# Linear attention and token/channel mixer on one core: another order of the first batches' operations, loads and constants

## The chip, the core and the metric

The kernel runs on one core of a Trainium2 chip. The metric is the device time of one execution in microseconds (us). The engines are TensorE (PE, with its weight loads PEld), VectorE (DVE), ScalarE (ACT), GpSimd (POOL) and SyncE (SP). Each takes its instructions in the order in which they were written, and a semaphore wait in front of one instruction holds everything behind it on that engine. DMAs are issued by SP (hardware queue, q1 in the profile) and POOL (software queue, q0 in the profile), and run on 16 DMA engines.

## What is computed

Cosformer attention over 8 batches, 8 heads, 576 positions and 64 channels a head, then one mixer layer:

```python
def phi(x, c, s):
    r = np.maximum(x, 0.0)
    return np.concatenate([r * c, r * s], axis=-1)
q_p, k_p = phi(q, cos_w, sin_w), phi(k, cos_w, sin_w)
kv = einsum('bhsf,bhsd->bhfd', k_p, v);  z = sum(k_p, axis=2)
x = einsum('bhsf,bhfd->bhsd', q_p, kv) / (einsum('bhsf,bhf->bhs', q_p, z) + 1e-06)
h = np.maximum(xt @ w_tok1, 0.0) @ w_tok2     # token mixing, xt = x transposed
u = x + h.transpose(0, 2, 1)
out = u + np.maximum(u @ w_ch1, 0.0) @ w_ch2  # channel mixing
```

## The kernel before

The 576 positions of a batch lie on 128 partitions, in J = 4 full row groups and a fifth, half-empty one (index 4); the half groups of two batches are put together in `u_tail` and go through the channel layer in pairs at the end. Work on heads is split in two halves of four heads, g = 0 and 1; g = 2 means both.

The stages of one batch, by the names of the operation list:

- `feat.b.t.j.g.f.E` (L289): one feature, relu(x * cos) or relu(x * sin) (f), of q or k, row group j, on engine E (D is DVE, A is ACT).
- `turn.b.i.g` (L305) transposes q's features on PE for two row groups (i = 0, 1) or for the fifth (i = 2), and `turno` (L314) copies them out of PSUM. Later batches use a DMA transpose instead, `turnx` (L319), issued by SP.
- `cast` (L300) rounds v to bf16 on DVE, ACT or POOL (P). `kvm` (L333) multiplies k's features with v, `kvo` copies the product out.
- `num` (L364) multiplies q's transposed features with kv; `numo` (L385) divides by the denominator on DVE (`x_out`, L373: a reciprocal and a multiplication) and gives x. From batch 2 on both heads' halves go together (`numf`, `numfo`).
- `mix` (L399) is the first token matmul, `mixo` its relu. `ux`, `ut`, `uto` (L414, L420) give u transposed; `um`, `uo` (L429, L436) give u itself, `tm`, `to` the fifth group's. `ubc`, `utr`, `utx` transpose u of later batches.
- `up` (L478) is the first channel matmul, in twelve blocks of columns, `upo` its relu; `dnw`, `dnj` the second, `o` (L508) adds u, and stores after every second row group.
- Loads: `ld.b.t.g.gate` (L220) issues two DMAs on SP, after the landing of the DMA that the gate names (v01 is v of batch 0, heads' half 1). The weights go through POOL's queue: `wt1` (w_tok1), `wt2` (w_tok2), `wu` (columns of w_ch1), `wd` (rows of w_ch2); `w2a` spreads w_tok2 to its place.

Batches 0, 1 and parts of 2 and 3 run by a list written out by hand or by a planner: `PLAN` (L16 to L55), a string of operations in program order, which the loop at L605 calls one after the other. The order of two operations on one engine is their order in the list. Ahead of the list stand the loads of batch 0 (L153: q, k, v's first half, v's second half), the memsets of constants, the sine and cosine tables, and 20 matmuls on zeros (`keep_warm`, L189) that keep PE busy while the first loads are under way. Behind the list come six rounds of `channel` for batches 2 to 7, with the attention of the next batches hooked in between, and one for the half groups of all pairs (`u_tail`).

Buffers that matter here: q and k each have two raw buffers (batches alternate), v has one; the features `qp` and `kp` have one buffer; PSUM has two slots of two banks (psA) and four of one (psM).

Of the kernel before, what the change touches and what calls it, by code (L numbers as in the profile page):

```python
# [681 lines left out]
```

## Time and profile before

| | us |
|---|---|
| median of 3 runs | 276.39 (275.82 to 276.94) |
| the profiled execution | 275.82 |
| its span, first to last instruction | 274.1 |
| PE busy | 260.9 (95% of the span) |
| DVE, ACT, POOL busy | 170.7, 114.4, 51.2 |
| first real transpose on PE | 8.88 |
| kvm of batch 0 starts | 17.63 |
| first mix of batch 0 | 21.54 |
| first `up` of batch 0 | 29.13 |
| kvm of batch 1, first half | 42.81 |
| last matmul ends | 270.43 |

The page gives the busy time of each engine, a strip of 40 slices of 6.85 us with busy tenths, the granted PE clock and the DMA share, then the chain that ended last, and the costliest groups of instructions. The trace behind it answers in more detail: a table by stretches of time, the waits of an engine with what ended them, the instructions in order of time, and the packets of each DMA queue in a stretch. An idle engine costs nothing unless it sets the end, so the strip is read first for the engine that is nearly always full, and then for where it is not.

### The profile page before, as it was taken

To read this page: it belongs to the slowest core of one execution; us is meant where nothing else is said; L and a number is where in the kernel's file an instruction comes from. 1 tells how busy PE (TensorE), PEld (TensorE's weight loads), DVE (VectorE), ACT (ScalarE), POOL (GpSimd) and SP (SyncE) were. 2 spreads that over 40 slices of the span, in tenths; PEclk is the share of its full clock that TensorE was granted. 3 is DMA by queue.
4 is the path that set the end of the run, shared out by engine and by line. 5 is a ranking of instruction groups with operands and counts; after the bars stand their busy time and mean duration, and the time that the engine had idled before them with its cause. 6 is when DMAs were issued, how large, how long until landed. Compare 5 with 4: busy or idle time off the path is not lost.

```text
span 274.1 us, 4680 instructions
## 1 busy us (share of the span) xinstructions
PE 260.9 (95%) x1846; PEld 134.5 (49%) x1846; DVE 170.7 (62%) x331; ACT 114.4 (42%) x181; POOL 51.2 (19%) x77
## 2 busy tenths in 40 slices
PE   7558999999999999999999999999999999999994
PEld 2257646445544554455445544554455444444443
DVE  4668889598773476947684869486738643323322
ACT  2653865377781339133913392338233201301300
POOL 5381060052030033600160017001100120000000
PEclk9959999999999999999999999999999999999999
DMA  6999999999899999999999968910990063003013
GB/s 204 332 151 258 311 199 218 366 356 202 256 256 200 362 366 363 152 230 281 347 158 266 306 215 137 250 57 1 177 243 4 2 124 125 0 17 138 0 44 110
DMA packets 79078, 53.36 MB, mean 195 GB/s; under 512 B 47824, under 2 KB 76496, under 8 KB 79056
## 3 DMA queue, kind: packets, MB, share of 16 engines
q1 hardware_dynamic: 74512, 48.77, 65.8%
q0 software_dynamic: 4144, 3.77, 9.4%
q10 hardware_dynamic: 400, 0.52, 0.5%
q8 instruction: 14, 0.23, 0.4%
q14 instruction: 8, 0.07, 0.1%
HBM read 35.85 MB, written 9.44 MB: 165 GB/s over the span
## 4 chain that ended last, share of the span: by engine, by line
PE 75%; DVE 0%; issue 0%
PE c_ps L562 26%; PE o_ps L579 26%; PE b L406 5%; PE c L485 4%; PE u L433 4%; PE o L497 4%; PE nf L357 3%; PE kv L327 3%; PE o_ps L571 1%; PE ut L461 1%; DVE u_tail L573 0%
## 5 line engine op out<-in xcount | busy, mean ns | idle before, releaser
L263 ACT ACTIVATE h<-c_ps 128x512 bf16<-128x512 f32 x52 | 31.0, 597 | 108.4 <-PE c_ps L562 64.2
L579 PE MATMUL o_ps<-wc,h 128*128 128x512 bf16 x324 | 71.9, 379 | 0.0
L562 PE MATMUL c_ps<-uT,wc 128*128 128x512 bf16 x288 | 70.4, 379 | 0.0
L579 PEld LDWEIGHTS <-h 128*128 128x128 bf16 x324 | 31.7, 98 | 38.2
L562 PEld LDWEIGHTS <-wc 128*128 128x128 bf16 x336 | 30.8, 98 | 32.6
L265 DVE TENSOR_SCALAR h<-c_ps 128x512 bf16<-128x512 f32 x32 | 22.0, 688 | 28.4 <-PE c_ps L562 28.4
L259 POOL CAST ub<-u 128x1024 bf16<-128x1024 f32 x14 | 15.1, 1076 | 124.4 <-DVE u L438 80.7
L582 DVE TENSOR_TENSOR u<-o_ps,u 128x512 f32<-128x512 f32 x24 | 16.5, 688 | 17.6 <-PE o_ps L579 17.6
L259 POOL CAST vbf<-vt 128x512 bf16<-128x512 f32 (+3 forms) x28 | 20.1, 753 | 22.3 <-PE c_ps L562 18.5
L296 ACT ACTIVATE qp<-qt,cos_t 128x512 bf16<-128x512 f32 x31 | 21.9, 713 | 5.0 <-DMA qt<-in_q_dram 5.0
L485 PE MATMUL c<-uT,wc 128*128 128x512 bf16 x96 | 23.1, 379 | 0.1
L497 PE MATMUL o<-wc,h 128*128 128x512 bf16 x96 | 22.3, 379 | 0.0
L296 ACT ACTIVATE qp<-qt,sin_t 128x512 bf16<-128x512 f32 x31 | 21.5, 711 | 0.7 <-DMA qt<-in_q_dram 0.7
L406 PE MATMUL b<-x,w 128*128 128x512 bf16 (+1 forms) x90 | 20.5, 355 | 1.0 <-DVE x L383 1.0
L383 DVE TENSOR_TENSOR x<-nf,den 128x512 bf16<-128x512 f32 x30 | 20.7, 691 | 1.0
L438 DVE TENSOR_TENSOR u<-u,x 128x1024 f32<-128x1024 f32 x16 | 19.4, 1220 | 1.7 <-PE u L433 1.7
L357 PEld LDWEIGHTS <-qpT 128*128 128x128 bf16 x320 | 15.4, 99 | 8.4 <-issue 0.4
L298 DVE TENSOR_SCALAR kp<-kt,cos_t 128x512 bf16<-128x512 f32 x30 | 17.9, 596 | 2.0 <-DMA kt<-in_k_dram 2.0
L298 DVE TENSOR_SCALAR kp<-kt,sin_t 128x512 bf16<-128x512 f32 x31 | 17.0, 557 | 0.0
L379 DVE TENSOR_SCALAR den<-nf 128x8 f32<-128x8 f32 x30 | 5.0, 166 | 18.4 <-PE nf L357 18.3
L433 PE MATMUL u<-B,w 128*128 128x512 bf16 x64 | 16.3, 379 | 0.0
L497 PEld LDWEIGHTS <-h 128*128 128x128 bf16 x96 | 9.0, 98 | 10.2
(89 smaller groups left out, 250.2 us busy)
## 6 DMA issues: line engine op xcount, KB each, us to landing
out_dram<-u SPq DMA_DIRECT2D x32, 256.0 KB, 2.6
qt<-in_q_dram SPq DMA_DIRECT2D x8, 640.0 KB, 8.6
kt<-in_k_dram SPq DMA_DIRECT2D x8, 640.0 KB, 7.2
qt<-in_q_dram SPq DMA_DIRECT2D x8, 512.0 KB, 7.5
kt<-in_k_dram SPq DMA_DIRECT2D x8, 512.0 KB, 6.0
vt<-in_v_dram SPq DMA_DIRECT2D x6, 640.0 KB, 9.2
vt<-in_v_dram SPq DMA_DIRECT2D x6, 512.0 KB, 8.1
wc<-in_moe_w_ch_dram POOLq DMA_DIRECT2D x4, 384.0 KB, 6.8
```

The source lines that it names most:

```text
L259: (nc.scalar.copy if eng == "A" else ENG[eng].tensor_copy)(dst, src)
L263: nc.scalar.activation(dst, src, AF.Relu)
L265: nc.vector.tensor_relu(dst, src)
L296: nc.scalar.activation(dst, src, AF.Relu, scale=tab)
L298: ENG[eng].tensor_scalar(dst, src, scalar1=tab, scalar2=0.0, op0=ALU.mult, op1=ALU.max)
L357: nc.tensor.matmul(nm[:, hh * (D + 1):(hh + 1) * (D + 1)], self.qpT[:, j * H + h, :], self.kv[:, h, :D + 1], start=(not eps or hh == 0), s ...
L406: nc.tensor.matmul(b1[:, mi], w1[:, col(self.c, j), mi * P:(mi + 1) * P], self.x[:, j, cs], start=(j == 0 and (g == 2 or mi == 0)), stop=( ...
L433: nc.tensor.matmul(ps[:, jj], w2[:, ki, 1 + 2 * g + jj, :], self.B1[:, ki, :], start=(ki == 0), stop=(ki == NT - 1))
L485: nc.tensor.matmul(ps, wc1[:, ki, mi * P:(mi + 1) * P], self.uT[:, :, ki, :], start=(ki == 0), stop=(ki == NCC - 1))
L497: nc.tensor.matmul(self.ps["o", j], self.h1[:, ki, j * P:(j + 1) * P], wc2[:, ki, :], start=(ki == 0), stop=(ki == NCH - 1))
L562: nc.tensor.matmul(c_ps, wc1[:, ki, mi * P:(mi + 1) * P], uT[:, :, ki, :], start=(ki == 0), stop=(ki == NCC - 1))
L579: nc.tensor.matmul(o_ps, h1[:, ki, j * P:(j + 1) * P], wc2[:, ki, :], start=(ki == 0), stop=(ki == NCH - 1))
```

## The change

The change gives the list another order, most of it in batches 0 and 1, and it moves constants and gates. Part by part:

- Ten memsets (`zero`, the clear of q's second buffer, `ones`, `eps_r`, two of `vbf`, two of `w1`, two of `w2`) go from POOL to DVE.
- The two index patterns (`iota`) are issued on POOL right after the first load; the identity is made where the list has the new word `mkid`.
- `ld.1.q.2` loses its gate v01 and stands first in the list, so SP issues it directly behind v of batch 0.
- w_tok2 comes first of the weights, gated by v01 (`wt2.v01`), behind one cast on POOL; w_tok1 follows after a second cast; then `wu.4`, `wu.0`, POOL's part of `w2a`, `wu.2`, `wu.8`.
- Batch 0's ten q features all come ahead of its k features, and its six groups of transposes ahead of `kvm.0.0`. Two features of batch 1's q stand on DVE ahead of `numo.0.0.1`.
- k of batch 1 is gated by `wu2` instead of q of batch 1. On POOL two `wd` are gated by k of batch 1, then one by `wu8`, one by v of batch 1; two casts of batch 1 follow. q of batch 2 comes before k.
- k of batch 4 is issued ahead of batch 3's DMA transposes; v of batch 4, and q gated by k of batch 3, ahead of the last stores of batch 1.

`FIRST = "S"` keeps batch 0's loads on SP; `ldp` is defined and not used. The diff, with the list up to batch 1's numerators and its last lines, first the old list:

```diff
-feat.0.q.2.2.0.D feat.0.q.0.2.1.D feat.0.q.1.2.0.A wt1.k02 feat.0.q.3.2.0.A feat.0.q.0.2.0.D feat.0.q.4.2.0.D
-feat.0.k.4.2.0.D wt2 feat.0.k.0.2.0.A feat.0.q.1.2.1.D turn.0.0.0 wu.4.4.k02 feat.0.k.4.2.1.D turn.0.0.1
-feat.0.k.2.2.1.A feat.0.k.0.2.1.D feat.0.k.1.2.1.A feat.0.q.4.2.1.D feat.0.k.3.2.0.A turn.0.2.0 turno.0.2.0.A
-turno.0.0.0.A cast.0.3.2.0.D feat.0.q.3.2.1.D feat.0.k.1.2.0.D feat.0.q.2.2.1.D turn.0.1.0 turno.0.1.0.A
-cast.0.0.3.0.P feat.0.k.3.2.1.D feat.0.k.2.2.0.D kvm.0.0 kvo.0.0.A cast.0.0.3.1.P cast.0.3.2.1.P kvm.0.1
-num.0.0.0 turno.0.0.1.D numo.0.0.0 w2a.0.A mix.0.0.0 num.0.1.0 w2a.1.P turn.0.1.1 num.0.2.0 ld.1.q.2.v01
-kvo.0.1.D num.0.0.1 turn.0.2.1 mix.0.1.0 wu.2.2.wt2 numo.0.1.0 turno.0.1.1.A mix.0.2.0 num.0.1.1 turno.0.2.1.A
-num.0.2.1 mix.0.3.0 numo.0.0.1 numo.0.2.0 mix.0.4.0 mixo.0.0.A wu.0.2.v01 wu.8.4 mix.0.0.1 feat.1.q.0.2.0.A
-numo.0.1.1 mix.0.1.1 ux.0.0 feat.1.q.0.2.1.A mix.0.2.1 mix.0.3.1 ux.0.3 numo.0.2.1 mix.0.4.1 ux.0.1 ut.0.1
-mixo.0.1.D ut.0.0 uto.0.0.A ut.0.3 um.0.0 feat.1.q.4.2.0.A feat.1.q.3.2.0.D feat.1.q.1.2.1.A uto.0.1.D
-up.0.2.0.2 up.0.3.0.2 feat.1.q.1.2.0.D ux.0.2 ut.0.2 turn.1.0.1 uo.0.0 feat.1.q.2.2.1.A ld.1.k.2.q12 uto.0.3.D
...
+ld.1.q.2 feat.0.q.4.2.0.D feat.0.q.1.2.0.A feat.0.q.4.2.1.D feat.0.q.2.2.1.A feat.0.q.0.2.0.D mkid
+feat.0.q.2.2.0.A feat.0.q.3.2.0.D feat.0.q.1.2.1.D feat.0.q.0.2.1.D turn.0.0.0 turn.0.2.1 feat.0.q.3.2.1.A
+feat.0.k.3.2.0.D turn.0.1.1 turno.0.1.1.D feat.0.k.4.2.0.A turn.0.2.0 feat.0.k.1.2.1.D feat.0.k.3.2.1.D
+turno.0.2.1.A cast.0.0.3.0.P wt2.v01 turn.0.0.1 turn.0.1.0 turno.0.0.0.A feat.0.k.2.2.0.A feat.0.k.0.2.1.A
+feat.0.k.4.2.1.D feat.0.k.2.2.1.D feat.0.k.0.2.0.A feat.0.k.1.2.0.D cast.0.3.2.0.D kvm.0.0 turno.0.1.0.D
+kvo.0.0.D num.0.1.0 turno.0.2.0.A num.0.2.0 numo.0.2.0 cast.0.0.3.1.P cast.0.3.2.1.A numo.0.1.0 num.0.0.0
+numo.0.0.0 kvm.0.1 kvo.0.1.D num.0.2.1 turno.0.0.1.A num.0.0.1 feat.1.q.1.2.0.D feat.1.q.2.2.1.A num.0.1.1
+feat.1.q.0.2.1.D wt1.k02 mix.0.0.0 wu.4.4.q02 numo.0.0.1 mix.0.0.1 mix.0.1.1 numo.0.1.1 mix.0.2.1 mix.0.3.1
+numo.0.2.1 wu.0.2.k02 mix.0.1.0 mix.0.2.0 feat.1.q.2.2.0.A mix.0.3.0 mix.0.4.0 ux.0.0 ux.0.1 mix.0.4.1 w2a.0.A
+mixo.0.1.A mixo.0.0.D w2a.1.P ut.0.0 uto.0.0.A tm.0 ux.0.2 to.0 ut.0.2 feat.1.q.1.2.1.A feat.1.q.0.2.0.D
+uto.0.2.D feat.1.q.3.2.1.D ut.0.1 uto.0.1.A um.0.0 uo.0.0 wu.2.2.v00 up.0.2.0.2 up.0.3.0.2 wu.8.4.v01 ux.0.3
+ut.0.3 turn.1.0.1 turno.1.0.1.D ld.1.k.2.wu2 feat.1.q.4.2.1.A feat.1.q.4.2.0.A turn.1.2.1 uto.0.3.A up.0.0.0.2
+up.0.2.2.4 up.0.3.2.4 up.0.8 upo2.0.1.D turno.1.2.1.A up.0.6 up.0.11 ld.1.v.0 upo.0.8.A ld.1.v.1.wu8
+feat.1.q.3.2.0.D up.0.4 upo.0.4.D feat.1.k.0.2.0.D feat.1.k.3.2.0.A up.0.1.0.2 up.0.0.2.4 feat.1.k.4.2.1.D
+upo.0.11.D feat.1.k.2.2.1.D upo.0.6.A wd.6.3.k12 feat.1.k.3.2.1.D up.0.1.2.4 upo2.0.0.D turn.1.1.1
+feat.1.k.1.2.1.A wd.0.3.k12 up.0.10 feat.1.k.1.2.0.A feat.1.k.2.2.0.D turn.1.0.0 feat.1.k.4.2.0.D wd.9.3.wu8
+um.0.1 cast.1.4.1.0.D feat.1.k.0.2.1.D wd.3.3.v11 upo.0.10.A turno.1.1.1.A turn.1.1.0 turno.1.1.0.A
+ld.2.q.2.wd0 turno.1.0.0.A up.0.5 upo.0.5.A cast.1.0.4.0.P cast.1.0.4.1.P turn.1.2.0 turno.1.2.0.D kvm.1.0
+kvo.1.0.A up.0.9 num.1.1.0 cast.1.4.1.1.P uo.0.1 ld.2.k.2.wd9 numo.1.1.0 kvm.1.1 up.0.7 upo.0.9.A kvo.1.1.A
...
+feat.3.k.3.2.0.A upo.1.8.A uo.2.1 ubc.2.1 feat.3.k.2.2.1.D feat.3.k.2.2.0.A cast.3.1.1.2.P dnj.1.3.0 dnj.1.2.0
+utx.2.1 dnj.1.3.1 dnj.1.2.1 feat.3.q.4.2.1.A turnx.3.4.1 dnj.1.0.1 o.1.0 dnj.1.1.0 dnj.1.1.1 cast.3.4.1.2.A
+ld.4.v.2 o.1.2 tm.2 ld.4.q.2.k32 o.1.3 to.2 o.1.1
...
-    nc.gpsimd.memset(zero, 0.0)
+    nc.vector.memset(zero, 0.0)
...
-    def load(b, t, hs=slice(0, H)):
+    def load(b, t, hs=slice(0, H), eng=nc.sync):
...
-            dmas.append(nc.sync.dma_start(
+            dmas.append(eng.dma_start(
...
-    for t, g in LOADS0:
-        d = load(0, t, heads(g))
+    for n, (t, g) in enumerate(LOADS0):
+        d = load(0, t, heads(g), nc.gpsimd if FIRST == "P" else nc.sync)
         landed[f"{t}0{g}"] = d[1]
...
+        if n == 0:
+            nc.gpsimd.iota(pos_i, pattern=[[2, JT]], base=-2, channel_multiplier=R)
+            nc.gpsimd.iota(par_i, pattern=[[0, 1]], base=0, channel_multiplier=1)
...
-    clear("q", 1, nc.gpsimd)
+    clear("q", 1, nc.vector)
...
-    make_identity(nc, ident)
...
-    nc.gpsimd.memset(ones, 1.0)
+    nc.vector.memset(ones, 1.0)
...
-    nc.gpsimd.memset(eps_r, 1e-6 / P)
+    nc.vector.memset(eps_r, 1e-6 / P)
...
-        nc.gpsimd.memset(t[:, :, :, D:], 1.0)
+        nc.vector.memset(t[:, :, :, D:], 1.0)
...
-        nc.gpsimd.memset(w1[:, i], 0.0)
+        nc.vector.memset(w1[:, i], 0.0)
...
-        nc.gpsimd.memset(w2[:, :, i, :], 0.0)
+        nc.vector.memset(w2[:, :, i, :], 0.0)
```

## The prediction

> **What bounds the kernel now.** I read the strip of 40 slices first, then the table by stage, the waits of PE, and the timeline of the first 30 us.
>
> ```profile
> PE   7558999999999999999999999999999999999994
> PEclk9959999999999999999999999999999999999999
> DMA  6999999999899999999999968910990063003013
> ```
>
> PE is full from the fifth slice on (about 27 us). Before it lie three poor slices, one of them at half clock. The DMA engines are full from the second slice to about 165 us, so early loads compete.
>
> ```profile
> 10.00:15.00 5.00, 1.23 (x16) 0.91 (x16) 4.36 (x8) 4.00 (x6) 3.76 (x5) 0.93 1.01 250
> 15.00:20.00 5.00, 3.20 (x51) 3.20 (x52) 3.49 (x5) 2.04 (x3) 4.05 (x5) 0.50 0.96 156
> 20.00:25.00 5.00, 3.95 (x74) 3.38 (x72) 3.86 (x11) 2.13 (x3) 1.71 (x3) 0.89 1.17 278
> 25.00:30.00 5.00, 4.85 (x38) 2.92 (x36) 4.10 (x8) 3.32 (x6) 0.00 (x0) 1.00 1.27 209
> ```
>
> Columns: stretch, its length, busy PE, PEld, DVE, ACT, POOL, clock, DMA share, GB/s. PE is idle for 3.77, 1.80, 1.05 and 0.15 us in these four, and the clock halves in the second. After 30 us PE loses about 0.3 us until the last store. So only the start can win, and all of it is won or lost by the moment at which PE becomes full.
>
> ```profile
> PE tr L311 <- DVE qp L298: 6.3, 3, 3.6
> PE b L406 <- DVE x L383: 1.0, 1, 1.0
> SPq L142 <- DMA qt<-in_q_dram: 11.9, 1, 11.9
> ```
>
> The first line is PE waiting for q features to transpose, the second the token mix waiting for x. The third is SP, between issuing batch 1's q (13.89 to 15.19) and its landing (27.1).
>
> ```profile
> 20.55 0.21 DVE L377 RECIPROCAL den<-nm 128x8 f32<-128x8 f32 x1 [2.06 <-PE nm L361]
> ...
> 22.24 0.21 DVE L377 RECIPROCAL den<-nm 128x8 f32<-128x8 f32 x1 [0.42 <-PE nm L361]
> ...
> 25.59 0.43 DVE L383 TENSOR_TENSOR x<-nm,den 128x256 bf16<-128x256 f32 x1
> ```
>
> The six normalisations (numo) of batch 0 are DVE's chain from 20.55 to 26.02. Each costs 0.88 us for two row groups (22.24 to 23.15, 24.54 to 25.39) and 0.54 for one. The mixes follow them; the last ends at 26.44 and `ut` starts at 26.66.
>
> **The change, part by part.**
>
> *Constants on VectorE.* Ten memsets leave POOL for DVE. DVE's rows are 0.48 us for 512 columns and 0.06 for one, so 0.0008 per column: zero 0.48, q's clear 0.48, ones 0.17, eps 0.06, vbf 2 x 0.13, w1 and w2 4 x 0.27, together 2.5 (2.7 by POOL's rows for the same memsets). DVE is idle for 2.63 us before q lands (6.93), which covers it; an overrun of 0.1 is taken up by the idle 2.04 us before k (10.64). `zero` comes 0.7 later, so the 20 warming matmuls end at 9.7 instead of 9.0. The first transposes need features that end at 9.5. Cost 0. If DVE's cover were gone, each 0.1 would move the q features, and those have 1 us to spare until k. The identity moves on POOL behind the iotas and is ready by about 2: 0.
>
> *All q features, then all transposes, first.* DVE: 6 x 0.42 from 6.93 = 9.5; ACT: 4 x 0.62 = 9.4. All 5 x 8 = 40 transposes are done by about 13.0 (the last two groups wait for PSUM slots freed by copies after k's landing). Of them 0.61 + 0.38 us ran at 22 to 23.4 before. What is late next is k. ACT has one k feature (11.35), two copies (0.5 and 1.0), three k features: 14.8. DVE has one k feature, a copy of 0.65, five k features and a cast.
>
> ```profile
> 12.23 0.48 DVE L298 TENSOR_SCALAR qp<-qt,sin_t 128x512 bf16<-128x512 f32 x1
> ...
> 15.70 1.04 DVE L298 TENSOR_SCALAR qp<-qt,sin_t 128x512 bf16<-128x512 f32 x1
> ...
> 14.63 2.58 POOL L259 CAST vbf<-vt 128x768 bf16<-128x768 f32 x3
> ```
>
> The same feature costs 0.48 alone and 0.83 to 1.04 beside POOL's casts. POOL casts twice instead of three times now; I charge 0.4 for each of three overlapped operations: DVE is done at 15.5. The Trainium skill, "SBUF — State Buffer", section "SBUF: two separate sides", calls the port pair of DVE and GpSimd an exclusive lock, where one side blocks wholly. By that rule an overlapped feature would wait out a whole cast of 0.86, which would put DVE's end near 16.8; the row shows less, and I go by the row.
>
> So kvm.0.0 ends at 16.0 instead of 18.9, kv is copied by 16.6, and the six num (0.66 us at half clock or 0.31 at full clock for two row groups) feed DVE from 17.2 (full clock) to 17.7 (half). DVE then has numo 0.54 + 0.88 + 0.88 and the kv copy 0.42: it is free at 19.9 to 20.4. Before, that point was 23.15. Gained so far: about 3 us of DVE's chain.
>
> *Batch 1's q loses its gate; weights come later.* This decides. In the new list, two features of batch 1's q stand on DVE directly ahead of numo.0.0.1, numo.0.1.1 and numo.0.2.1; whatever q1 is late by, those three, four mixes and everything behind on PE are late by. Let L be q1's landing. From L: two features 0.87, numo 0.88 and 0.88, two mixes 0.43, four mixes of group 0 0.86, two `ux` 0.44, one mix 0.22 = L + 4.58. Then 0.1 for B's last evacuation, and `ut`, `tm`, `ux`, `ut`, `ut`, `um` (0.43, 0.43, 0.22, 0.43, 0.43, 0.86 at full clock): the first channel matmul (`up`) starts at L + 7.5. The old kernel starts it at 29.13 without having done `tm`, so the same work stands at 29.13 + 0.43 = 29.56. Gain = 29.56 - 7.5 - L = 22.1 - L, and no more than 22.1 - 20.1 = 2.0, since DVE itself is free only at 20 or so.
>
> What is L? Before, q1 was issued at 13.89 into a queue full of weights:
>
> ```profile
> q0 software_dynamic: 98, 0.10, 65.6%
> q1 hardware_dynamic: 87, 0.09, 31.9%
> ```
>
> That is 19 to 20 us: packets, MB, share of 16 engines. Weights (q0) and loads (q1) go packet for packet, but a weight packet takes some 0.11 us and a load's 0.05; alone, loads do 335 packets per us (344 in 11 to 12). Now q1's 1056 packets (summed by one-us stretches, 17 to 27) stand directly behind v's, which end at 12.7. w2 waits for v's landing (13.2, my estimate; 13.8 before, with w1 in between), is issued 13.2 to 13.95, and its packets start at 14.3: q1 has 536 done. Beside w2's 256 packets 256 more (to 16.9), beside w1's 128 large ones (0.28 us each) 128 (to 19.5), the last 136 beside wu4 at 120 per us: 20.6. Tails of single engines cost up to 1 us more (k1: last bulk at 33.0, landed 34.4). L = 21.6: gain 0.5. Bounds: 20.1 (q1 gets ahead further) and 24.7 (as starved as before, when its first half landed).
>
> The Trainium skill speaks against expecting more here: "DMA: Bandwidth & Descriptors", section "Issuing engines are not separate DMA queues", says that DMAs of all issuing engines run on the same 16 engines and interleave. By that rule the reordering moves q1 forward only by moving weights back; by the rows the bytes until about 30 us are also the same.
>
> Are the weights late, then? w1 (issued 14.9 to 16.75 on POOL, behind one cast) ends at 19.5 and lands by about 20.3; the first mix wants it at 21 to 22. w2 lands at 17.5 and w2a has until 26. wu4 ends at 22.8, wu0 24.5, wu2 26.2 and lands by 27; up.0.2 wants it at 29.1 (27.6 at best). Nothing waits, with 0.6 to 2 us to spare.
>
> *Batch 1's list (30 to 62 us).* k1 waits for wu2 as above, is issued at 27 as before (27.18) and lands near 33.6. POOL's queue then has wd6, wd0, wd9, and wd3 waiting for v's second half, with both casts of v that kvm.1.0 and kvm.1.1 need behind it. v1 has 790 packets done when wd's come (34.6); 266 at 120 per us plus the tail: 38.2. wd3 39.0, cast 1.12: 40.1. kvm.1.0 comes one `up` (0.86) earlier in the list: 42.81 - 0.86 - 0.5 = 41.45. Spare 1.3 us: cost 0. The q2, k2, v2 loads come 0 to 3 us earlier: 0.
>
> *Batches 2 and 3, and the fifth batch's loads.* SP gets k's two issues ahead of batch 3's transposes (0.6 us each) and q's ahead of the last stores. Batch 3's transposes had been issued from 75.66 with 4.6 us to land, for a PE that wants them at 94.9: over 10 us to spare, cost 0. PE's work is the same matmuls, and it is full: 0.
>
> Sum: 0.5 us off the profiled execution (275.82 us, span 274.1). The median of the runs is 0.57 above that execution, so 276.39 - 0.5 = **275.9 us**.
>
> **Rivals.**
>
> 1. *q1 gets through early* (L at 20.1 to 20.8) and the clock stays up, since PE is busy 1.5 us between 11.2 and 14.6 instead of 1.2. Gain 1.3 to 2.0, and up to 0.3 where PE's late stalls go too: about 274.6. For it: loads alone at 335 per us. Against: 98 to 87 packets beside weights.
> 2. *q1 is starved as before.* From 13.9 to 17 q1 had no packets at all while weights flowed. If loads behind v stop when w2 starts and L is 24.7, the gain is 22.1 - 24.7 = -2.6: 279.0, slower. It decides from L = 23.5 on. Against: v's queue is already running then.
> 3. *A wait further on*: v's second half lands after 39.5, and POOL holds kvm.1.0's cast behind wd3; each us later costs one. If k1 starts 2 us later, v shares with all wd's, lands at 42, and the cast ends at 44: 2.5 lost, less 0.5: 278.4. For it: k2 before took 12.3 us to land beside wd's.
>
> **Numbers.** Faster or slower by over 0.5% (1.4 us) is about what a measurement can tell. Forecast 0.40 (275.0 to 277.8; its own range 275.2 to 276.6), rival 1 0.27, rivals 2 and 3 together 0.33. The range takes in rival 1 down to 274.0 and most of rivals 2 and 3: 274.0 to 279.0.
>
> **What would show it.** Right: q1 landing at 21 to 22.3, DVE waiting there for q1 by 1 to 2 us ahead of numo.0.0.1; transposes all before 13.5; first `up` near 28.6 to 29.1; no PE wait after. Wrong: w1 or wu2 ending a PE wait, POOL's cast ending kvm.1.0's wait, DVE still at memsets at 6.93.

## The result and the profile after

The changed kernel takes 277.69 us (median of 4 runs, 277.51 to 277.99) where the kernel before takes 276.38 beside it (275.82 to 276.94). The ratio is 1.0048, with a 95% interval of 1.0026 to 1.0071: slower by about 1.3 us, where the prediction had 0.5 us faster. The profiled execution of the changed kernel took 277.99 us, with a span of 276.2 (before: 275.82 and 274.1).

The strip of 40 slices of the changed kernel:

```profile
PE   6747996999999999999999999999999999999994
PEclk9995999999999999999999999999999999999999
DMA  6999999999999999999989887930890053003013
```

The half clock has moved by one slice, from the third to the fourth, and the seventh slice (41 to 48 us) now has a 6 where the old kernel had a 9. So there are two places to look at: the start, and something after 41 us. The table by stage, with the columns of the one shown before:

```profile
10.00:15.00 5.00, 2.97 (x51) 2.56 (x51) 4.26 (x8) 4.35 (x8) 1.85 (x2) 1.00 1.09 355
15.00:20.00 5.00, 2.42 (x68) 2.19 (x65) 4.21 (x11) 4.22 (x6) 4.98 (x8) 1.00 1.05 207
20.00:25.00 5.00, 3.48 (x37) 2.56 (x34) 3.09 (x8) 0.00 (x0) 1.49 (x3) 0.61 1.08 146
25.00:30.00 5.00, 5.00 (x30) 3.10 (x29) 1.91 (x4) 1.93 (x4) 0.00 (x0) 0.71 1.20 179
```

Between 10 and 15 us PE does more (2.97 us busy instead of 1.23), and at full clock. From 21.1 to 27.9 it runs at half clock, and that is where the matmuls of the token mix lie. The waits of PE between 9 and 50 us (times in us: total, count, longest):

```profile
PE nm L362 <- DVE kv L264: 2.3, 2, 1.8
PE kv L332 <- DVE kp L303: 2.3, 1, 2.3
PE b L411 <- DMA w<-in_moe_w_tok_dram: 1.5, 1, 1.5
...
PE tr L316 <- DVE qp L303: 0.6, 1, 0.6
```

The wait for q features has shrunk from 6.3 us to 0.6, as the reordering was to do. Two others have come in its place: the mixes wait 1.5 us for w_tok1, and kv of batch 1 waits 2.3 us for a k feature of DVE. PE's timeline has both, with their price:

```profile
19.77 0.29 PE L362 MATMUL nm<-kv,qpT 128*128 128x65 bf16 x4 [1.79 <-DVE kv L264]
...
22.19 4.00 PE L411 MATMUL b<-x,w 128*128 128x256 bf16 x18 [1.52 <-DMA w<-in_moe_w_tok_dram]
...
30.54 0.81 PE L490 MATMUL c<-uT,wc 128*128 128x512 bf16 x3
...
45.37 0.81 PE L332 MATMUL kv<-vbf,kp 128*128 128x65 bf16 x20 [2.28 <-DVE kp L303]
```

The first `up` (L490) stands at 30.54; the old kernel had the same work done at 29.56 (29.13 and 0.43 of `tm`, as in the prediction). So 0.98 us is lost by then in this execution (other executions of the same start are compared below). At kv of batch 1 the start is 2.56 us later than before (45.37 against 42.81), and at the first matmul of the later rounds (c_ps, L567) 2.21 us later (93.07 against 90.86). From there on the distance stays 2.2 until the last matmul (272.63 against 270.41): what the change does behind that point, the fifth batch's loads among it, costs and gains nothing.

### The profile page after: what moved, and what is told of

It is laid out like the page before. It is cut to its first block, busy times and chain, and to the rows that moved or that the text cites. A ratio compares the mean times of both kernels' runs of the same rounds, so it can differ in the third digit from the quotient of the medians.

```text
span 276.2 us, 4685 instructions
## 1 busy us (share of the span) xinstructions
PE 261.3 (95%) x1846; PEld 134.4 (49%) x1846; DVE 167.4 (61%) x333; ACT 116.4 (42%) x187; POOL 49.5 (18%) x69
## 4 chain that ended last, share of the span: by engine, by line
PE 88%; DMA 5%; DVE 4%; issue 1%; POOL 1%; SPq 0%; ACT 0%
PE c_ps L567 26%; PE o_ps L584 25%; PE o L502 8%; PE b L411 7%; PE c L490 6%; PE u L438 5%; PE kv L332 3%; DMA vt<-in_v_dram 3%; PE nf L362 3%; DMA w<-in_moe_w_tok_dram 2%; DVE kp L303 2%; PE ut L466 1%; PE o_ps L576 1%; PE uT L428 1%; DVE h L270 1%
## 5 line engine op out<-in xcount | busy, mean ns | idle before, releaser
L567 PE MATMUL c_ps<-uT,wc 128*128 128x512 bf16 x288 | 70.4, 379 | 0.0
L584 PEld LDWEIGHTS <-h 128*128 128x128 bf16 x324 | 31.7, 98 | 38.2
L567 PEld LDWEIGHTS <-wc 128*128 128x128 bf16 x336 | 30.8, 98 | 32.6
L264 POOL CAST ub<-u 128x1024 bf16<-128x1024 f32 x14 | 14.9, 1067 | 103.8 <-DVE u L443 54.8
L264 POOL CAST vbf<-vt 128x512 bf16<-128x512 f32 (+3 forms) x30 | 21.7, 757 | 50.9 <-DMA vt<-in_v_dram 39.9
L301 ACT ACTIVATE qp<-qt,sin_t 128x512 bf16<-128x512 f32 x32 | 22.6, 711 | 2.6 <-DMA qt<-in_q_dram 2.6
L411 PE MATMUL b<-x,w 128*128 128x512 bf16 (+1 forms) x90 | 22.2, 387 | 1.5 <-DMA w<-in_moe_w_tok_dram 1.5
L490 PE MATMUL c<-uT,wc 128*128 128x512 bf16 x96 | 22.7, 379 | 0.0
L301 ACT ACTIVATE qp<-qt,cos_t 128x512 bf16<-128x512 f32 x29 | 20.5, 711 | 3.9 <-DMA qt<-in_q_dram 3.9
L388 DVE TENSOR_TENSOR x<-nf,den 128x512 bf16<-128x512 f32 x30 | 20.7, 691 | 1.0
L362 PEld LDWEIGHTS <-qpT 128*128 128x128 bf16 x320 | 15.3, 98 | 10.5 <-issue 2.1
L303 DVE TENSOR_SCALAR kp<-kt,sin_t 128x512 bf16<-128x512 f32 x30 | 18.5, 629 | 0.0
L332 PE MATMUL kv<-vbf,kp 128*128 128x65 bf16 x320 | 12.0, 193 | 3.8 <-DVE kp L303 2.3
L303 DVE TENSOR_SCALAR kp<-kt,cos_t 128x512 bf16<-128x512 f32 x28 | 15.0, 544 | 0.8 <-DMA kt<-in_k_dram 0.8
```

The source lines that it names most:

```text
L264: (nc.scalar.copy if eng == "A" else ENG[eng].tensor_copy)(dst, src)
L301: nc.scalar.activation(dst, src, AF.Relu, scale=tab)
L303: ENG[eng].tensor_scalar(dst, src, scalar1=tab, scalar2=0.0, op0=ALU.mult, op1=ALU.max)
L362: nc.tensor.matmul(nm[:, hh * (D + 1):(hh + 1) * (D + 1)], self.qpT[:, j * H + h, :], self.kv[:, h, :D + 1], start=(not eps or hh == 0), s ...
L411: nc.tensor.matmul(b1[:, mi], w1[:, col(self.c, j), mi * P:(mi + 1) * P], self.x[:, j, cs], start=(j == 0 and (g == 2 or mi == 0)), stop=( ...
L490: nc.tensor.matmul(ps, wc1[:, ki, mi * P:(mi + 1) * P], self.uT[:, :, ki, :], start=(ki == 0), stop=(ki == NCC - 1))
```

## The experiments

All kernels ran beside the kernel before on their own chip, so ratios are compared. The kernel before had medians of 276.1 to 276.6 in the groups of runs, and of 275.46 in the one of `e9_front`, `e10_tail` and `e11_split`. The milestones come from one profiled execution each (us from the span's start): the first `up` of batch 0, the start of kv of batch 1, and the first c_ps. "After" is the time between first `up` and c_ps. The kernel before starts this stretch at 29.56; e4, e7, e9, e10, e13 and e14 have other work ahead of that `up` than the changed kernel, so theirs isn't given.

| kernel | median, us | ratio to before (95%) | first up | kv of batch 1 | c_ps | after |
|---|---|---|---|---|---|---|
| before | 276.38 | 1 | 29.13 | 42.81 | 90.86 | 61.30 |
| changed | 277.69 | 1.0048 (1.0026 to 1.0071) | 30.54 | 45.37 | 93.07 | 62.53 |
| e2_casts | 275.72 | 0.9987 (0.9968 to 1.0007) | 30.08 | 43.01 | 90.71 | 60.63 |
| e11_split | 276.45 | 1.0021 (1.0000 to 1.0041) | 29.50 | 44.09 | 91.79 | 62.29 |
| e10_tail | 277.95 | 1.0078 (1.0050 to 1.0107) | 30.01 | 44.73 | 92.44 | |
| e14_tail_casts | 276.77 | 1.0007 (0.9989 to 1.0024) | 31.49 | 43.97 | 91.87 | |
| e8_q1gated | 280.21 | 1.0138 (1.0115 to 1.0161) | 34.80 | 48.57 | 96.27 | 61.47 |
| e4_q1early | 275.50 | 0.9990 (0.9969 to 1.0010) | 28.57 | 42.25 | 90.13 | |
| e7_constants | 276.37 | 1.0008 (0.9991 to 1.0026) | 29.30 | 42.98 | 90.88 | |
| e3_w1first | 276.77 | 1.0030 (1.0013 to 1.0046) | 30.89 | 44.98 | 92.68 | 61.79 |
| e1_warm | 277.46 | 1.0049 (1.0022 to 1.0076) | 29.06 | 44.03 | 93.29 | 64.23 |
| e5_both | 276.23 | 1.0005 (0.9983 to 1.0028) | 28.61 | 41.91 | 90.64 | 62.03 |
| e6_swap_casts | 277.26 | 1.0040 (1.0017 to 1.0063) | 27.76 | 43.16 | 92.54 | 64.78 |
| e9_front | 278.17 | 1.0086 (1.0053 to 1.0119) | 31.55 | 44.15 | 92.09 | |
| e13_front_gates | 276.36 | 1.0004 (0.9986 to 1.0023) | 30.09 | 42.68 | 90.28 | |
| e12_inputs | 274.60 | 0.9935 (0.9913 to 0.9957) | 29.29 | 42.01 | 89.73 | 60.44 |
| e15_cold_inputs | 275.82 | 0.9992 (0.9973 to 1.0011) | 30.31 | 43.00 | 90.76 | 60.45 |
| e16_inputs_pool | 277.58 | 1.0046 (1.0024 to 1.0068) | 28.15 | 42.83 | 92.08 | 63.93 |

The theory at the outset had two parts: the wait at kv of batch 1 comes from POOL's casts of v, which hold up DVE's k feature, and the late start comes from w_tok1's landing and the half clock that follows. The rival was that the start is all, and the wait further on only a consequence.

### The wait at kv of batch 1

DVE, POOL and PE of the changed kernel around 40 us; the first line is the one feature that matters:

```profile
40.06 2.72 DVE L303 TENSOR_SCALAR kp<-kt,sin_t 128x512 bf16<-128x512 f32 x1
```

```profile
39.70 0.77 POOL L248 DMA_DIRECT2D wc<-in_moe_w_ch_dram  x1 [1.38 <-DMA vt<-in_v_dram]
40.48 2.57 POOL L264 CAST vbf<-vt 128x1024 bf16<-128x1024 f32 x3
```

The same feature takes 0.48 us a moment earlier. POOL waits for v's second half, issues its last w_ch2 load at 39.70 (0.77 us) and then casts twice 1024 columns, until 42.50; the feature ends at 42.79. The k features queued behind it end at 45.31, and kv starts at 45.37.

**e2_casts** takes only those two casts from POOL, to places where ACT is idle.

```diff
-... upo.0.5.A cast.1.0.4.0.P cast.1.0.4.1.P turn.1.2.0
+... feat.1.k.1.2.0.A cast.1.0.4.0.A feat.1.k.2.2.0.D ... wd.3.3.v11 cast.1.0.4.1.A upo.0.10.A ... upo.0.5.A turn.1.2.0
```

> The changed kernel with the two large casts of batch 1's v (halves 0 and 1, 1024 columns each) taken from POOL and put on ACT, where ACT waits for PE (near 38.3 and 39.7 us). Theory 'lock': the k feature that took 2.72 us beside POOL's casts takes under 1, kvm.1.0's wait falls from 2.3 us to 0.5 or less, and the time falls by 1.5 to 2.0 us, to 275.7 to 276.2. Theory 'loads': k and v of batch 1 are simply late, the feature starts late whatever POOL does, kvm.1.0 starts at 45.4 again, 277.7. The first up stays at 30.5 under both.

Its features and POOL's work at the same place:

```profile
39.21 1.22 DVE L303 TENSOR_SCALAR kp<-kt,sin_t 128x512 bf16<-128x512 f32 x2
40.36 1.21 DVE L270 TENSOR_SCALAR h<-c 128x1024 bf16<-128x1024 f32 x1
```

```profile
39.44 0.77 POOL L248 DMA_DIRECT2D wc<-in_moe_w_ch_dram  x1 [2.57 <-DMA vt<-in_v_dram]
40.21 0.47 POOL L264 CAST vbf<-vt 128x256 bf16<-128x256 f32 x1
```

Two features now take 1.22 us together, though POOL still issues its load beside them; kv of batch 1 waits 0.38 instead of 2.28, and the time is 0.9987 of before instead of 1.0048: the loss is gone, although the start in this profile is still half a microsecond late.

**e11_split** asks how long POOL keeps DVE out: the two casts of 1024 columns are cut into four of 512.

```diff
-cast.1.0.4.0.P cast.1.0.4.1.P
+cast.1.0.2.0.P cast.1.2.2.0.P cast.1.0.2.1.P cast.1.2.2.1.P
```

> The changed kernel, with POOL's two casts of 1024 columns ahead of kv of batch 1 cut into four of 512. Theory A (DVE's feature is held until POOL's instruction in hand ends, and gets its turn between two of them): the feature that took 2.72 us takes 1.3 us or less, kv of batch 1 waits 0.8 to 1.5 us instead of 2.28, time 276.4 to 277.2. Theory B (POOL's queued casts follow one another without letting DVE in): the feature still takes 2.2 to 3.0 us, the wait is 2.0 to 2.7, time 277.3 to 278.2. Rival (the feature was slow for a cause that has nothing to do with POOL's casts, such as its own place in the queue): as B in time, with the feature outside of the casts' span.

```profile
40.34 2.81 POOL L264 CAST vbf<-vt 128x512 bf16<-128x512 f32 x5
40.55 2.88 DVE L303 TENSOR_SCALAR kp<-kt,cos_t 128x512 bf16<-128x512 f32 x2
```

The first of these two features runs from 40.55 to 42.90, the four casts from 40.34 to 42.61, one directly behind the other. So cutting the casts doesn't free the feature earlier: it lasts to the end of the four as it did to the end of the two, which is theory B in the mechanism (kv waits 2.0). The time doesn't decide: 276.45 us lies in theory A's range, but the kernel before had 275.46 beside it, and the interval of the ratio (1.0000 to 1.0041) overlaps with the changed kernel's.

**e10_tail** gives the old first half the new second half: the list of before up to `um.0.0`, with batch 1's q behind v again and the constants on DVE, and the changed list from there on, with the casts on POOL. **e14_tail_casts** is the same with the two casts on ACT, at the places of e2. The change to the kernel before, at the seam:

```diff
-mixo.0.1.D ut.0.0 uto.0.0.A ut.0.3 um.0.0 feat.1.q.4.2.0.A feat.1.q.3.2.0.D feat.1.q.1.2.1.A uto.0.1.D
+mixo.0.1.D ut.0.0 uto.0.0.A ut.0.3 um.0.0 feat.1.q.1.2.0.D feat.1.q.2.2.1.A feat.1.q.2.2.0.A
+tm.0 ux.0.2 to.0 ut.0.2 feat.1.q.1.2.1.A uto.0.2.D feat.1.q.3.2.1.D uto.0.1.A uo.0.0 up.0.2.0.2 up.0.3.0.2
...
```

> The mirror image: the earlier list through batch 0's normalisation, with batch 1's q behind v of batch 0 again, then the changed list from there on, POOL's casts of v for kv of batch 1 included; the constants are set on DVE. Theory: the start is the earlier one (first up at 29.0 to 29.8), and kv of batch 1 waits 1.5 to 2.5 us, with one of its last features on DVE at 1.2 us or more beside POOL's casts instead of 0.48; time 277.0 to 278.2. Rival (the second half costs nothing by itself, it only came late): a wait under 0.6 us and 276.1 to 276.6.

```profile
38.05 2.71 DVE L303 TENSOR_SCALAR kp<-kt,sin_t 128x512 bf16<-128x512 f32 x1
```

```profile
38.45 2.57 POOL L264 CAST vbf<-vt 128x1024 bf16<-128x1024 f32 x3
```

> The earlier first half with the changed second half, and v's two late casts on ACT instead of POOL. Theory (POOL's casts beside the last k features are the whole cost of the second half): the feature that took 2.71 takes 0.7 or less, kv of batch 1 waits 0.5 or less (1.78 beyond its matmuls), time 275.6 to 276.5 (277.95 with the casts on POOL). Rival (the second half's load order costs too): 276.8 to 278.

With the old start the same feature again takes 2.71 us and kv waits 1.6: the second half brings its loss along, whatever the start is. With the casts on ACT that feature takes 0.48, PE has no wait for a k feature at kv, and the ratio falls from 1.0078 to 1.0007:

```profile
39.52 0.48 DVE L303 TENSOR_SCALAR kp<-kt,sin_t 128x512 bf16<-128x512 f32 x1
```

The absolute median of e14 is above the theory's range by 0.3, but the median of the kernel before was 1.1 us higher in that group too.

### The start

**e8_q1gated** puts back the gate of batch 1's q, in the changed list: the prediction's formula said that whatever q is late by, the first `up` is late by.

```diff
-ld.1.q.2 feat.0.q.4.2.0.D ... cast.0.0.3.0.P wt2.v01
+feat.0.q.4.2.0.D ... cast.0.0.3.0.P wt2.v01 ld.1.q.2.v01
```

> The changed kernel with batch 1's q gated by v of batch 0 again, as in the kernel before. This tests the term that the prediction hung on: the two q features ahead of numo.0.0.1 on DVE hold the mixes until q lands at L, and the first up starts at L + 7.5. With the gate, q's packets go beside the weights and L is 24 to 27; the first up then starts at 31.5 to 34.5, and the kernel is slower than the changed one: 278.7 to 281. A theory that says the early q pushes the weights back (w1 at 22.1) expects w1 to land at 19 to 20 here and the kernel to be no slower than 277.7.

```profile
26.01 0.48 DVE L303 TENSOR_SCALAR qp<-qt,cos_t 128x512 bf16<-128x512 f32 x1 [5.84 <-DMA qt<-in_q_dram]
```

```profile
24.54 0.58 PE L411 MATMUL b<-x,w 128*128 128x256 bf16 x2 [2.94 <-DMA w<-in_moe_w_tok_dram]
27.79 3.28 PE L411 MATMUL b<-x,w 128*128 128x256 bf16 x16 [2.66 <-DVE x L388]
```

With L = 26.0 the formula gives 33.5, and the first `up` stands at 34.80; the rest is the clock, since sixteen mixes took 3.28 us where eighteen take 2.13 at full clock (e1 below). So the gate's removal is what makes this order work at all.

**e4_q1early** does that one part alone in the kernel before (`ld.1.q.2` first, without its gate), **e7_constants** the ten memsets alone.

> The kernel before with one part of the change alone: batch 1's q issued right behind batch 0's v, with no gate. Theory 'two waits' (late w1 and the locked feature, both from where weights and casts stand on POOL): q1 by itself costs nothing here, since w1 is still first of the weights; q1 lands near 17 to 20 instead of 27.1, the first mix stays at 21.5, the time at 276.4 within 0.4. Theory 'bytes': q1's 1.18 MB ahead of the weights push w1 and w_tok2 back, the first mix waits, and this kernel is slower by 1 us or more, 277.4.

> The kernel before with one part of the change alone: the ten memsets on DVE instead of POOL. All theories that name a late load or a lock expect nothing: DVE has the memsets done by 5.8 us and q lands at 6.9 to 7.4; 276.1 within 0.3 of the kernel before. A theory that puts part of the loss on the later start of the warming matmuls (2.27 instead of 1.77) expects 276.6 or more.

Neither can be told from no change: 0.9990 and 1.0008. Constants on DVE cost nothing that shows, as predicted.

**e3_w1first** issues w_tok1 ahead of the first cast and of w_tok2, so that the mixes need not wait for it.

```diff
-cast.0.0.3.0.P wt2.v01 ... wt1.k02 mix.0.0.0
+wt1.k02 cast.0.0.3.0.P wt2.v01 ... mix.0.0.0
```

> The changed kernel with w_tok1 issued first on POOL, at the landing of k, as in the kernel before, and w_tok2 behind it. Theory 'w1 late': w1 lands by 17, the first mix starts at 20.7 to 21 when num is done instead of 22.2, and the first up at 29.5 instead of 30.5; the clock still falls at 21, because PE idles at 18 to 19.8 as before, so the mixes stay slow. Time 276.7 if kvm.1.0's wait does not grow, 277.7 if it does. Theory 'bytes': v and w_tok2 come later by what w1 comes earlier (about 2 us), kvm.0.0 or B then waits, and the time is 277.7 or more.

The wait for w is gone, but the first `up` stands at 30.89, not at 29.5: DVE's cast of v takes 1.65 us beside POOL's issue of w_tok2 and its cast (kv of batch 0 waits 0.9 for it), and x comes later (0.8). It gains a little further on, where kv of batch 1 waits 1.5 instead of 2.28. The time, 276.77, is the one that theory 'w1 late' expected, but not by its way: that was luck.

**e1_warm** leaves the loads alone and keeps PE busy with eleven more matmuls on zeros (fillers) ahead of the mixes, so that the clock comes back.

```diff
-... kvm.0.1 kvo.0.1.D ... wt1.k02 mix.0.0.0
+... kvm.0.1 kw.6 kvo.0.1.D ... wt1.k02 kw.5 mix.0.0.0
```

> The changed kernel with 11 more matmuls on zeros, in the two stretches where PE idles at 18 to 22 us (six after kvm.0.1, five ahead of the first mix); nothing else moves. Theory 'clock': the first 18 mix matmuls took 4.0 us at half clock and should take 2.0; the first up moves from 30.5 to 28.4 (w_ch1's second part lands only then), and kvm.1.0's wait for DVE (2.3 us) shrinks, because DVE gets past the two k features before POOL's casts start at 40.5: 275.0 to 276.2 us. Theory 'loads': kvm.1.0 starts when its k features and casts are there, at about 45.4 whatever PE does before; its wait grows from 2.3 to 4.4 us and the time stays at 277.7. Theory 'list': PE's order alone costs the time, 277.7 with no change of the wait.

```profile
23.20 2.13 PE L411 MATMUL b<-x,w 128*128 128x256 bf16 x18
...
44.03 0.81 PE L332 MATMUL kv<-vbf,kp 128*128 128x65 bf16 x20 [2.42 <-DVE kp L303]
```

The eighteen mixes take 2.13 us instead of 4.00 and the first `up` comes 1.5 us earlier, and the time does not move (1.0049). At kv of batch 1 DVE's feature again waits for POOL's casts, and those for v; kv still starts 1.34 us earlier than in the changed kernel, and this rest is lost behind it: after the wait the clock is halved from 45.2 to 48.6 us. The same happens in e16 below (43.4 to 46.9).

The half clock of the start needs a closer look, since it is not the same from one profiled execution to the next. In e2, whose list ahead of the first `up` is the changed kernel's, the clock (third number from the right) falls at 17 us, before the two gaps of PE that the changed kernel's timeline showed:

```profile
16.00:17.00 1.00, 0.89 (x29) 0.89 (x29) 0.27 (x3) 0.63 (x1) 1.00 (x2) 0.98 0.88 150
17.00:18.00 1.00, 1.00 (x22) 0.99 (x19) 0.96 (x3) 0.68 (x2) 1.00 (x3) 0.50 1.32 199
```

| kernel | half clock from | to | first `up` |
|---|---|---|---|
| changed | 21.1 | 27.9 | 30.54 |
| e2, same start | 17.0 | 27.2 | 30.08 |
| e15, same start | 17.2 | 27.4 | 30.31 |
| e11, same start | 15.3 | 25.6 | 29.50 |
| e16, same start | 16.1 | 23.0 | 28.15 |
| e1, with fillers | 14.5 | 21.3 | 29.06 |
| e5, with fillers | 15.7 | 19.2 | 28.61 |
| e12, with fillers | 14.7 | 21.6 | 29.29 |
| before | 14.3 | 21.1 | 29.13, to be compared as 29.56 |

So the changed start is between 0.98 late and 1.41 early, by the execution. The fillers don't keep the clock from falling; with them it comes back sooner, ahead of the mixes in all three.

### Both together, and what was missing

**e5_both** is e1 and e2 together. **e6_swap_casts** is e2 with w_tok1 ahead of w_tok2 on POOL.

> The changed kernel with the 11 extra matmuls on zeros of e1 and the two casts on ACT of e2 together. Theory 'two losses in a row' (the slow start of the mixes, and then the k features of batch 1 that POOL's casts lock out): e2 alone took 2.0 us off, e1 alone moved the first up by 1.5 us (30.5 to 29.1) but lost it again at kvm.1.0 (wait 2.4 us) and to a clock that fell after that wait. With both, the gain at the first up (1.0 us against e2's 30.1) should be kept: 274.5 to 275.0. Theory 'inputs': kvm.1.0 cannot start before 43.0, where v's second half and the casts let it, so the time stays at e2's 275.7.

> The changed kernel with e2's casts on ACT and w_tok1 ahead of w_tok2 on POOL, both still behind v's landing. Theory 'w1 late': w1 lands at about 19 instead of 22, the first mix starts when num is done (20.7) and not at 21.7 to 22.2; half clock or not, the first up moves by 1 us, to 29.1 or before, and the time to 274.7. Theory 'clock': the wait for w1 was only a part of PE's idle time, the clock falls as before, the mixes take 4 us, and of the 1 us at most half is left at the first up: 275.2 to 275.7. If w_tok2 now is late (it has to be spread by 25), ut waits and the time is over 275.7.

Both missed. They have early starts (28.61 and 27.76) and give them back afterwards: e5 waits 0.73 for h and 0.66 for kv's copy, both on ACT, which got to its features of k only at 35.9, when k had landed, and then cast v until 40.25; e6 waits 0.9 for the last of its w_ch1 weights, 1.6 for h, 0.7 for kv's copy. A PE that comes earlier meets inputs that come when they did.

**e9_front** is the mirror of e10: the changed first half up to `uo.0.0`, and the old list from there on.

> The changed kernel's list through the copy of batch 0's first normalised half, then the earlier list from there on: k of batch 1 again behind the q of batch 1, v behind the first w_ch1 load, the ACT and DVE casts of v as they were, the fifth batch's loads as they were. Theory (two costs, one in each half of the list): the start is still late, first matmul of the up projection at 30.0 to 31.0 (30.54 in the changed kernel), for the weights' landing and the half clock lie in the first half; kv of batch 1 waits 0.6 us or less (2.28), since no two POOL casts lie beside its last features; time 275.8 to 276.9, the start's loss alone. Rival (all of the loss comes from the start): 277.4 to 278.0. Second rival (all of it from the second half): 276.1 to 276.5 with the first matmul of the down projection's first half level with the kernel before, 90.9.

It missed by more than a microsecond: 278.17, though kv of batch 1 waits no more than 0.2. SP's queue in this kernel and in **e13_front_gates**, which differs from it by two gates:

```diff
-wu.2.2.wt2 ... ld.1.k.2.q12
+wu.2.2.v00 ... ld.1.k.2.wu2
```

```profile
17.64 1.28 SPq L143 DMA_DIRECT2D kt<-in_k_dram  x2
31.64 1.26 SPq L143 DMA_DIRECT2D vt<-in_v_dram  x2
```

```profile
27.28 1.28 SPq L143 DMA_DIRECT2D kt<-in_k_dram  x2
28.73 2.69 SPq L143 DMA_DIRECT2D vt<-in_v_dram  x4
```

> The changed kernel's first half and the earlier second half again, with the two gates of the changed kernel kept: k of batch 1 behind the second w_ch1 load (it had been issued at 17.64, beside the token weights), that load behind v. Theory (the kernel with the earlier second half lost by k's early transfer on top of the start): k is issued at 27 to 29, c no longer waits 0.6 for its first weight, the down projection's first half starts within 0.8 us of the kernel before (90.86; it was 92.09), time 276.0 to 277.0. Rival (late start and half clock are the whole cost whatever follows): 277.2 to 278.2.

In e9 the early q released k at 17.64, beside the token weights; `up` then waited 0.6 for its first weights, and v went out 2.9 us later. With the gates of the changed kernel it is 276.36, a ratio of 1.0004. So the changed first half with the old second half costs nothing that shows, and e9's loss came from how the cut was made.

**e12_inputs** is e5 with k and v of batch 1 released earlier. **e15_cold_inputs** leaves out e12's fillers, **e16_inputs_pool** is the changed kernel with the earlier k and v alone.

```diff
-ld.1.k.2.wu2 ... ld.1.v.0 upo.0.8.A ld.1.v.1.wu8
+ld.1.k.2.wu0 ... ld.1.v.0 upo.0.8.A ld.1.v.1
```

> The changed kernel with the filler matmuls in the start and v's casts on ACT (as in the run that had both), and with k of batch 1 released by the first w_ch1 load instead of the second, v's second half no longer held for the last w_ch1 load. Theory (what was gained in the start was given back because k and v of batch 1 came no earlier): k is issued 1.5 to 3 us earlier (27.89), v's second half is cast before 39 (39.44), the waits for h and for kv's copy shrink from 0.73 and 0.66 to 0.3 or less, kv of batch 1 starts before 41.5, time 274.8 to 275.8. Rival (w_ch1 and w_ch2 weights share the same bytes per second, so what k and v gain they lose): c waits for a weight by 0.6 us or more, 276 to 277.

> The last kernel but for the filler matmuls: v's two late casts on ACT, k of batch 1 released by the first w_ch1 load and v's second half not held. Theory (casts off POOL and earlier k and v are what counts, the half clock at the mixes is paid back before kv of batch 1): no wait over 0.5 at kv of batch 1, 274.4 to 275.6. Rival (the mixes at half clock cost what the fillers saved, 1 to 1.5 us): 275.7 to 276.8.

> The changed kernel with k of batch 1 released by the first w_ch1 load and v's second half not held, nothing else: POOL keeps its two casts. Theory (the casts hold DVE's feature wherever they lie beside it, so earlier inputs only move the wait): a k feature of 2 us or more beside POOL's casts, 276.5 to 277.6. Rival (the casts come before the last k features and are done in time): no feature over 1.4 us, kv of batch 1 waits 0.6 or less, 275 to 276.

e12 is faster than both kernels: 274.60, a ratio of 0.9935 (0.9913 to 0.9957). k goes out at 26.48, 1.4 us earlier than in e5 (27.89), and the waits for h and for kv's copy on ACT are gone; PE's line at kv of batch 1 in e12:

```profile
42.01 0.81 PE L332 MATMUL kv<-vbf,kp 128*128 128x65 bf16 x20 [0.17 <-DVE kp L303]
```

kv itself didn't start before 41.5 as expected; this execution's start was 0.7 us later than e5's (29.29 against 28.61). The stretch from first `up` to c_ps fell from 62.03 to 60.44. In e15 the rival won: that stretch is as short (60.45), but the start is a microsecond later and 275.82 us are the result. e16 went as the theory had it (a feature of 2.19 us beside the casts, 277.58), in spite of its early start (28.15). The three edits, each alone and together, as ratios:

| v's casts on ACT | k, v earlier | fillers | ratio |
|---|---|---|---|
| no | no | no (changed kernel) | 1.0048 |
| no | no | yes (e1) | 1.0049 |
| no | yes | no (e16) | 1.0046 |
| yes | no | no (e2) | 0.9987 |
| yes | no | yes (e5) | 1.0005 |
| yes | yes | no (e15) | 0.9992 |
| yes | yes | yes (e12) | 0.9935 |

While POOL's casts stand in the way, neither of the others moves the time. With the casts gone, one of the two alone still shows nothing, and both together bring 0.5%. Fillers and earlier k and v without the casts' move weren't tried.

## Why the prediction was wrong

- **The bound.** "Only the start can win" hid the losing: the new list lost 2.3 us after 30 us. It didn't hold for winning either: e12 is 0.27 us ahead of the kernel before at the first `up` and 1.13 at c_ps. The 0.3 us that the prediction read is PE's idle time in the table, where busy time runs to the modelled ends of overlapping matmuls. By the distances between the starts of matmuls the kernel before loses some 1.2 us from the first `up` to c_ps, and e2 some 0.5 (estimates from the traces).
- **Constants, identity, transposes.** Right: e7 shows 1.0008 for the constants, and the transposes are done by 13.4 (13.0 forecast). The six normalisations started at 17.05 (17.2 to 17.7 forecast), and kv of batch 0 ended at 15.9 (16.0 forecast).
- **q of batch 1.** That what q is late by the first `up` is late by was borne out (e8), but L was not. q landed at 17.1, not at 21.6, because the loads had the DMA engines to themselves for longer: POOL waited 0.79 us for v before it issued w_tok2 at 14.18, and the packets of that load began only 1.7 us later. From 5 to 16 us the two queues of the changed kernel stand so (packets, MB, share of 16 engines):

```profile
q1 hardware_dynamic: 3527, 3.95, 107.4%
q0 software_dynamic: 4, 0.00, 0.3%
```

  That is 0.36 MB per us for the loads. From 17.2 on DVE set the moment (its two features of q began at 19.63), which is the limit of "DVE itself is free only at 20 or so". From there the formula gives 27.1 for the first `up`; it came at 30.54, because its terms hold no wait for weights and no half clock.
- **"Nothing waits" for the weights.** Wrong: w_tok1 landed at 22.06, not 20.3, 1.8 us late. It was issued at 16.05 to 17.15 (14.9 to 16.75 forecast) and took 5 us beside the first w_ch1 loads. PE waited 1.52 us, and the mixes fell into the half clock, which the prediction priced nowhere after 20 us: they took 4.00 us instead of 2.13 (e1). That made the first `up` 0.98 late instead of 0.5 early in this execution. The wait for w_tok1 isn't shown as what brought the clock down: most of it (20.7 to 22.2) lies behind the fall at 21.1, and in the other executions of this start the clock had fallen by 17.2.
- **What that late start costs in the end.** Nothing that can be measured: the same first half gives 1.0004 with the old second half (e13) and 0.9987 with the casts on ACT (e2). One reason is that it is not late in every execution (28.15 to 30.54, against 29.56). The old kernel also has small waits of its own after its `up` (61.30 us to c_ps, where 60.4 is possible); that a PE which comes later is spared them is my reading and wasn't tested by itself. The start is a cost where nothing else is late: 0.6% between e15 and e12, which differ by the fillers alone.
- **"Spare 1.3 us: cost 0" at kv of batch 1.** This is the step that failed, and as far as the times can tell it is the whole loss. It asked only when POOL's cast would be done (40.1 forecast) and not what the casts do to DVE beside them. In the changed list two casts of 1024 columns lie beside the last k features; in the old list it is one, beside DVE's own cast of v. PE waited 2.28 us there for DVE's feature, where the sum had 0. e2 takes the two casts away and the loss with them; e10 brings them with the changed second half and has the loss, and e14 takes them out of that again.
- **The rule that was set aside.** The prediction had the row of 0.83 to 1.04 us for a feature beside a cast and went by it, against the exclusive lock of the Trainium skill, "SBUF — State Buffer", section "SBUF: two separate sides". The runs side with the lock: 2.72, 2.71 and 2.34 us for a feature of 0.48. They go beyond one instruction, the unit that the page names: the feature waited through the load's issue and two casts, or through four casts. The row that I went by was misread: those two features began 0.25 and 0.30 us into a cast of POOL and ended 0.28 after its end, so they waited out what was left of it. The trace of before had two more rows that I passed over:

```profile
14.05 1.73 DVE L298 TENSOR_SCALAR kp<-kt,cos_t 128x512 bf16<-128x512 f32 x1
```

```profile
39.76 1.51 DVE L259 CAST vbf<-vt 128x1024 bf16<-128x1024 f32 x1
```

```profile
39.61 1.12 POOL L259 CAST vbf<-vt 128x1024 bf16<-128x1024 f32 x1
```

  The first is a feature that waited through the issue of a load and the first of POOL's three casts (14.63 to 15.49). The second is DVE's own cast of v, which takes 0.68 in e13; here it lay beside POOL's cast of the third row. At the start the charge of 0.4 for each of three operations still came out (DVE was done at 15.4, 15.5 forecast), since POOL's casts lay apart there.
- **Rivals.** Rival 3 named the place (kv of batch 1, behind the last w_ch2 load) and nearly the size, for another reason: POOL's wait for v's second half ended at 39.7, not at 42. That was luck. Rival 1's first condition (q by 20.8) came true, but the clock did not stay up, and the gain did not come. Rival 2 fell, and e8 shows what it would have cost: 1.0138.
- **Fifth batch's loads.** Right: 2.21 us of distance at 93 us, 2.22 at the last matmul.

## What to carry over

When an operation is moved to another engine or another place, ask what runs beside it on VectorE and GpSimd, and price a short VectorE operation beside GpSimd casts at what is left of the cast, here up to two or four casts in a row, not at its own duration times a factor. A kernel with PE full from some point on has several limits lying within a microsecond of each other (here the casts, the landing of k and v, the clock at the mixes): an edit that lifts one can show nothing until the others are lifted too, so edits that measure as zero alone are worth trying together. When a list is cut in two for an experiment, look at the gates across the cut first. Before a milestone of one profiled execution is explained, compare it with other executions of the same start.

## What was not expected of the hardware

- A DVE feature of 0.48 us was held up to 2.72 us by POOL and ended 0.29 us after POOL's last large cast in the three kernels whose rows are shown (42.50 and 42.79, 42.61 and 42.90, 40.47 and 40.76), whether POOL did two casts or four. It did not wait for POOL's last cast, of 256 columns, which followed directly. At the start of the kernel before, three casts of 768 columns followed one another as closely, and there a feature came out after each of them (1.73, 1.04 and 0.83 us). What decides when DVE gets its turn isn't shown.
- The clock fell without a long idle time. In the changed kernel the two gaps were 1.79 and 1.52 us, with 0.9 us of matmuls between them. The table by microsecond (18 to 23 us, the clock is the third number from the right):

```profile
18.00:19.00 1.00, 0.00 (x0) 0.00 (x0) 0.96 (x3) 0.95 (x2) 0.98 (x2) 1.00 0.97 151
19.00:20.00 1.00, 0.23 (x8) 0.23 (x8) 1.00 (x3) 0.96 (x1) 1.00 (x2) 1.00 0.89 145
20.00:21.00 1.00, 0.68 (x23) 0.58 (x19) 1.00 (x3) 0.00 (x0) 1.00 (x3) 1.00 0.85 86
21.00:22.00 1.00, 0.00 (x0) 0.00 (x0) 0.93 (x4) 0.00 (x0) 0.49 (x1) 0.53 0.95 123
22.00:23.00 1.00, 0.81 (x4) 0.58 (x5) 0.96 (x3) 0.00 (x0) 0.00 (x0) 0.50 1.14 166
```

  In all 18 profiled executions the clock changes a multiple of 3.41 us after its last change. In the changed kernel it fell at 21.05, and in the 3.41 us before that PE was busy for 1.25 us, or 37%. Worked out in the same way for the first 60 us of all the traces, PE was busy for 28 to 50% of the 3.41 us ahead of each fall and for at least 83% ahead of each return; in two cases, 45 and 47% did not bring it down.
- Where the half clock lies differs between profiled executions of the same start (the table under e1), and the first `up` with it by 2.4 us. One trace's milestones before 30 us are good to no more than that, and the verdicts above rest on the times of all runs.
